# Fixing VectorE's order in the opening of an attention and GEGLU kernel, and storing its first values from SyncE

## The chip, the cores and the metric

The kernel runs on one core of a Trainium2 chip. A core has five engines that each work through their own list of instructions in order and meet at semaphores: TensorE (PE, matrix products), VectorE (DVE, elementwise work on whole tiles), ScalarE (ACT, activations and copies), GpSimd (POOL) and SyncE (SP, here only a queue that issues transfers). ACT and POOL issue transfers too, from the same list as their other work. The metric is device time in microseconds for one execution; the number of a version is the median of its runs.

## The reference

With S = 2048 tokens, D = 512 channels, F = 1792 hidden channels, 32 heads of 16 channels, all float32:

```python
q, k, v = split(x @ wqkv)                     # 32 heads of 16
idx = pos[:, None] - 2 * arange(8)[None, :]   # 8 keys, every second token back
attn = softmax(where(idx >= 0, einsum(q, k[idx]) / 4, -1e9))
a = einsum(attn, v[idx]) @ wo
b = (gelu(x @ w_gate) * (x @ w_up)) @ w_down
g = sigmoid((x * gate_w).sum(-1))
out = g * a + (1 - g) * b
```

A token attends only to tokens of its own parity (even or odd), so the two parities, 1024 tokens each, are independent of each other.

## The kernel before

**Stages.** The kernel does parity 0, then parity 1. Each parity has: the products for keys and queries, the products for values, 14 steps of the feed-forward part (`ffn`, f = 0 to 13), and the attention of four units of eight heads, which runs on VectorE in between (`scores`, `softmax`, `mix`), pulled in by credit as PE's work is written down.

**Seven products.** A product of x with a weight is cut into 2 x 2 blocks on both sides and done with seven block products instead of eight. The operands are blocks (`a11`, `a12`, `a22`, `b11`, `b12`, `b21`, `b22`) and sums of them: on the side of x, s1 = a21 + a22, s3 = a11 - a21, s2 = s1 - a11, s4 = a12 - s2 (`sum_x`, L237 to L242); on the side of the weight t3 = b22 - b12, t2 = b11 + t3 up to the signs in the code, t4 and t1 (`combine_b`, L230 to L233, for keys; `make_v`, L157 to L185, for values). For keys and queries the order of the products is in `KEYS` (L449): a11·b11, a12·b21, s2·t2, s3·t3, a22·t4, and later s1·t1 and s4·b22.

**Two halves of a number.** Every operand is split in a rounded `hi` (written by ACT, L86 or L126, or by a DVE cast) and a rest `lo` = value - hi (DVE, L87, in `split`). A block product is hi·hi + lo·hi + hi·lo over two channel chunks (kc = 0, 1): six matmuls for each of four token tiles (t = 0 to 3), 24 in all, 512 columns wide for keys (L458, `key_mm`), 258 for values (L345, in `values`). So before PE can do the third product, DVE must have done, for each kc, three sums of x, one split of s2, two sums of weights and one split of t2, and ACT the two `hi` between them.

**The opening.** L1053 to L1066 load and split the first blocks. Then stand, in the order of the code: the first two key products (L1078 to L1085); `take_first` (L317 to L326), which copies the finished tile out of PSUM, t = 0 and 2 by DVE, t = 1 and 3 by ACT, and stores it with two transfers from SP; two steps of `make_v` (the split of the value weights b11 and b21); the operands of s2·t2 (L1095 to L1101); the value products 0 and 1 (L1102); the splits of s3 and t3; `third(2)`, `third(3)`, `third(4)` (L1108 to L1139), which do the third to fifth key product; and `values(0, ..., range(2, 7))` (L1170), the other five value products.

**Stores of values.** In `values`, `store` (L354) sends a tile of 128 x 256 to DRAM: 16 transfers in each parity, four of them after value product 1, eight after product 5, four after product 6. For parity 0 they stand in ACT's list, for parity 1 in SP's.

**Zeros.** L1142 to L1144 write 16 small blocks of zeros to DRAM from POOL, after `third(4)`.

**What sets the order.** The code above is not the order in which an engine gets its instructions. The framework's scheduler puts each engine's instructions in an order of its own, by dependences, priorities and an estimate of durations. Two calls bind it: `keep_in_program_order(ins)` keeps marked instructions of an engine in the order of the code among themselves, and `paced` (L574) ties an instruction behind the last matmul written so far. Before the change only the first casts (L1051) are marked. Transfers of SP's and ACT's queues share eight semaphores in turn, and most of them wait in the program for the transfer eight places before them.

**Parity 1.** `keys` (L414) writes the key products of parity 1 and pulls their operands step by step out of `prepare`, which begins with `urgent` (L253 to L268): the same operands of s2·t2 as in the opening, then the splits of s3.

Of the kernel before, what the change touches and what calls it, by code (L numbers as in the profile page):

```python
# [13 lines left out]
OP = mybir.AluOpType  # L14
# [30 lines left out]
def tile_gated_mix(ctx: ExitStack, tc: tile.TileContext, xt, wqkv, wff, wo, out):  # L45
# [36 lines left out]
    def split(eng, hi, lo, raw, copy=None, pinned=False):  # L82
        if copy:
            copy(hi, raw)
        else:
            nc.scalar.activation(hi, raw, AF.Copy)  # L86
        ins = eng.tensor_tensor(lo, raw, hi.bitcast(F32), op=OP.subtract)  # L87
        if pinned:
            tc.keep_in_program_order(ins)


    KS, VS, QS, OS, WS, DS = {}, {}, {}, {}, {}, {}
# [64 lines left out]
    def make_v():  # L157

        def parts(n):
            split(nc.vector, *VO[n], VR[n])  # L160
            VS_W[n] = dram.tile([2, P, VW], F32, name=f"vw{n}")
            keep_v.append(n)

        def sub(o, x, a, b):
            nc.vector.tensor_tensor(VR[x], VR[a], VR[b], op=OP.subtract)
            VR[o] = VR[x]

        parts("b11")
        yield
        parts("b21")  # L170
        yield
        sub("t1", "b11", "b12", "b11")
        parts("t1")
        yield
        parts("b22")
        yield
        sub("t3", "b12", "b22", "b12")
        sub("t2", "b22", "b22", "t1")
        parts("t2")
        yield  # L180
        sub("t4", "b21", "b21", "t2")
        yield
        for n in "t3", "t4":
            parts(n)
            yield  # L185
# [67 lines left out]
    def urgent():  # L253

        room_b("t2")
        for kc in range(2):
            for n in "s1", "s3", "s2":
                sum_x(kc, n)
            split_s("s2", kc)
            yield  # L260
            combine_b("t3", "b12", "b22", "b12", kc)
            combine_b("t2", "b11", "t3", "b11", kc, OP.add)
            split_b("t2", kc)
            yield
        MADE.add("t2")
        for kc in range(2):
            split_s("s3", kc)
            yield  # L268
# [48 lines left out]
    def take_first(ps, jj, copy):  # L317

        if not KQ:
            KQ.append(pool.tile([P, 3 * NP - 1, UC], F32, name="kq"))  # L320
        st = tl(next(stages))[:, :CU].rearrange("p (a d) -> p a d", a=2)
        two = ps.rearrange("p (a c d) -> p c a d", a=2, c=2)
        copy(KQ[0][:, NP - 1 + jj::NP], two[:, 0])
        copy(st, two[:, 1])
        for a, t in enumerate((KS[0, 0][1, W:], QS[0, 0][1])):
            nc.sync.dma_start(t.rearrange("(p j) d -> j p d", j=NP)[jj], st[:, a])  # L326

# [5 lines left out]
    def values(par, bg, step, ks=range(7)):  # L333

        C, Z_, PS, US, ST = {}, {}, {}, {}, {}

        def mm(ps, t, a, b, start):
            ts = slice(t * P, (t + 1) * P)
            for kc in range(2):
                ah, al = XOP[a, kc]  # L340
                for i, (x, w) in enumerate(((ah, 0), (al, 0), (ah, 1))):
                    first = start and kc == i == 0

                    n = 512 if first and a == "s1" else WQ
                    LAST[:] = [nc.tensor.matmul(ps[:, :n], x[:, ts], VO[b][w][:, kc * WQ:kc * WQ + n], start=first,  # L345
                                                stop=(kc == 1 and i == 2), skip_group_check=True)]

        def stage():
            return tl(next(stages))[:, :512]

        def copy(o, i):
            nc.scalar.activation(o, i, AF.Copy)  # L352

        def store(st, jj, hh):  # L354
            queue = nc.sync if par else nc.scalar
            queue.dma_start(rows(VS[par, hh][:, W:], jj), st.rearrange("p (c d) -> p c d", c=2))

        for k, (a, b) in enumerate((("a11", "b11"), ("a12", "b21"), ("s1", "t1"), ("s4", "b22"), ("s2", "t2"),
                                    ("s3", "t3"), ("a22", "t4"))):
            if k not in ks:  # L360
                continue
            for t in range(BT):
                if k == 0:
                    C[t] = bank(f"acc{t}") if par else bank("p")
                elif k == 1 and not par:
                    Z_[t] = C[t]
                elif k == 2:
                    Z_[t] = bank("p")
                    if not par:
                        C[t] = bank(f"acc{t}")  # L370
                        copy(C[t][:, :WQ], VB.pop(t))
                ps = Z_[t] if 0 < k < 4 else C[t]
                mm(ps, t, a, b, k in (0, 2))
                if k == 0 and par:
                    Z_[t] = bank("p")
                    copy(Z_[t][:, :WQ], ps[:, :WQ])
                elif k == 0:
                    VB[t] = tl("s" if t else "r")[:, :WQ]
                    copy(VB[t], ps[:, :WQ])
                elif k == 2:  # L380
                    PS[t] = stage()
                    copy(PS[t][:, :CU], ps[:, :CU])
                elif k == 3:
                    copy(PS[t][:, CU:], ps[:, :CU])
                elif k == 4:
                    US[t] = stage()
                    copy(US[t][:, CU:], ps[:, :CU])
                elif k == 5:
                    copy(US[t][:, :CU], ps[:, :CU])
                    nc.vector.tensor_tensor(PS[t], PS[t], US[t], op=OP.add)  # L390
                    store(PS[t][:, CU:], t, 1)
                    store(PS[t][:, :CU], BT + t, 1)
                else:
                    if k == 1 or not par:
                        ST[t] = stage()
                    jj, st = (t, ST[t][:, :CU]) if k == 1 else (BT + t, ST[t][:, CU:])
                    copy(st, ps[:, :CU])
                    copy(z[:, par, jj:jj + 1], ps[:, CU:WQ - 1])
                    store(st, jj, 0)
                next(bg, None)  # L400
                pull((0.77, 0.75)[par])
            step(k)
        for _ in bg:
            pass
        if 6 not in ks:
            return
        done.add((par, 1))
        en = pool.tile([P, 64], F32, name="en")[:, :NP]
        nc.scalar.activation(en, z[:, par], AF.Exp, scale=-1.0)
        nc.vector.tensor_scalar_add(en, en, 1.0)  # L410
        nc.vector.reciprocal(g[:, par], en)
        nc.vector.tensor_scalar(gc[:, par], g[:, par], -1.0, 1.0, op0=OP.mult, op1=OP.add)
# [160 lines left out]

    def paced(ins):  # L574

        if not PACING[0]:
            return ins
        tc.add_manual_dep(ins.ins, LAST[-1].ins.name, mybir.DependencyInfo(mybir.DependencyClass.Sync,
                          mybir.DependencyReason.SCHED_ONLY), reason="pace")
        return ins  # L580
# [472 lines left out]
    for kc in range(KC):  # L1053
        name, i = ("b11", "b21")[kc // 2], kc % 2
        if not i:
            room_b(name)
        first = ((0, P), (P, 512 - P)) if not kc else ((0, 512),)
        raw = QR[name, i] = spare[i] if kc > 1 else tl("rt")
        (nc.sync if kc else nc.scalar).dma_start(raw, wqkv[0, kc // 2, :, i * 512:i * 512 + 512])
        for a, n in first:  # L1060
            o = kc // 2 * 512 + a
            nc.sync.dma_start(XR[i][:, o:o + n], xt[0, :, kc, a:a + n])
        for c in first:
            split_x(0, 0, kc, (c,), None if kc else in_order)
            if not c[0]:
                split(nc.vector, *QO[name, i], raw)  # L1066
    set_x(0)
    for kc in range(2):
# [14 lines left out]
    for kc in range(2):  # L1083
        for t in range(BT):
            key_mm(Z_[t], t, *KEYS[1], (kc,), False)  # L1085
    for t in range(BT):
        take_first(Z_[t], t, first_copy[t % 2])
    room_v(*SMALL)
    made = make_v()
    for _ in range(2):  # L1090
        next(made)
    room_b("t2")
    S1.update((kc, pool.tile([P, UH, NP, W], F32, name="lg", bufs=2).rearrange("p h j w -> p (h j w)"))
              for kc in range(2))
    for kc in range(2):  # L1095
        for n in "s1", "s3", "s2":
            sum_x(kc, n)
        split_s("s2", kc)
        combine_b("t3", "b12", "b22", "b12", kc)
        combine_b("t2", "b11", "t3", "b11", kc, OP.add)  # L1100
        split_b("t2", kc)  # L1101
    values(0, iter(()), lambda k: None, range(2))  # L1102
    room_b("t3")
    for kc in range(2):
        split_s("s3", kc)
# [30 lines left out]
    next(made)  # L1136
    for f in range(2):
        fetch(f)
    third(4)  # L1139
    done.add((0, 0))  # L1140
    PACING[0] = True
    for t in (*KS.values(), *VS.values()):  # L1142
        for c in range(2):
            paced(nc.gpsimd.dma_start(t[c, :W], zero))  # L1144

    def first():
        for _ in range(2):
# [87 lines left out]
```

## Time and profile before

| | us |
|---|---|
| median of 3 runs | 623.32 (622.73 to 623.71) |
| the profiled execution | 622.21 |
| its span, first to last instruction | 620.4 |

| engine | busy us | share of the span |
|---|---|---|
| PE | 597.5 | 96% |
| DVE | 540.7 | 87% |
| ACT | 432.5 | 70% |
| POOL | 110.5 | 18% |

The mean granted clock of PE over the span is 0.983 of full speed. A row of the timeline gives the start and duration of an instruction (or of several equal ones, with their count), the engine, the line of the code, the operation, the tile written and the tiles read, and in brackets how long the engine sat idle before it and what ended that. A "q" behind an engine's name is that engine's list issuing a transfer. Line numbers are those of the kernel before. A row of the windows gives, for a stretch of time, each engine's busy time with its number of instructions, the granted clock of PE, and the load of the transfer engines.

### The profile page before, as it was taken

The numbers are of one execution on the slowest core, as the hardware profiler recorded it, in microseconds if no ns is written. First come the engines' busy times: TensorE is split into PE (matmuls) and PEld (weight loads), VectorE is DVE, ScalarE is ACT, GpSimd is POOL, SyncE is SP. The second block draws the span as 40 slices with busy tenths as digits, with TensorE's granted clock in tenths as the row PEclk, the third lists the DMA queues.
The fourth block names the chain that finished last, engine by engine and source line by source line (L and its number), as shares of the span: only waits on it lengthen the run. The fifth ranks groups of instructions, "written<-read, shape, count | busy, mean of one in ns | idle before, by whom it ended". The sixth has DMA issues, their size and how long they took to land.

```text
span 620.4 us, 8250 instructions
## 1 busy us (share of the span) xinstructions
PE 597.5 (96%) x2743; PEld 494.7 (80%) x2743; DVE 540.7 (87%) x637; ACT 432.5 (70%) x755; POOL 110.5 (18%) x129
## 2 busy tenths in 40 slices
PE   8798987999999999999889999999999999999997
PEld 7686876888878888887669988888888888888886
DVE  6937965999969998899978999899989998999892
ACT  6756489667797777886857666676687668686732
POOL 0006066111111111111200176011111111121300
PEclk9989988999999999999979999999999999999999
DMA  8677799988776967799849999968867896888824
GB/s 306 221 216 191 221 243 294 214 218 245 218 192 165 293 200 225 194 276 314 257 138 277 330 262 248 313 172 233 234 169 185 229 257 165 208 216 213 113 49 169
DMA packets 94697, 137.78 MB, mean 222 GB/s; under 512 B 8640, under 2 KB 58944, under 8 KB 94655
## 3 DMA queue, kind: packets, MB, share of 16 engines
q1 hardware_dynamic: 70510, 102.98, 50.6%
q0 software_dynamic: 19504, 31.79, 29.5%
q10 hardware_dynamic: 4640, 2.49, 1.4%
q8 instruction: 21, 0.34, 0.2%
q14 instruction: 22, 0.17, 0.1%
HBM read 69.83 MB, written 44.66 MB: 185 GB/s over the span
## 4 chain that ended last, share of the span: by engine, by line
PE 65%; DVE 13%; issue 8%; ACT 6%; DMA 6%; SPq 1%; ACTq 0%; POOL 0%; DVEq 0%; POOLq 0%
PE p L725 31%; PE acc L767 9%; PE p L767 8%; PE acc L458 7%; PE p L992 5%; PE p L345 2%; PE acc L992 2%; DVE prod L551 1%; PE acc L345 1%; DVE raw L242 1%; DMA raw<-xt 1%; DVE prod L511 1%; DMA vs<-hl 1%; DVE lg L514 1%; DMA r<-wff 1%
## 5 line engine op out<-in xcount | busy, mean ns | idle before, releaser
L725 PE MATMUL p<-S,g 128*128 128x512 f32 x672 | 170.6, 391 | 0.5 <-ACT s L730 0.5
L725 PEld LDWEIGHTS p<-S,g 128*128 128x128 f32 x672 | 126.7, 189 | 27.2 <-ACT s L730 0.9
L725 PE MATMUL p<-A,g 128*128 128x512 f32 x504 | 127.2, 391 | 4.6 <-ACT c L736 4.6
L725 PEld LDWEIGHTS p<-A,g 128*128 128x128 f32 x504 | 94.2, 188 | 25.5 <-ACT c L736 5.9
L511 DVE TENSOR_TENSOR prod<-kq 128x2048 f32<-128x2048 f32 x32 | 72.9, 2279 | 2.7 <-DMA kq<-kq 2.6
L551 DVE TENSOR_TENSOR prod<-v,lg 128x2048 f32<-128x2048 f32 x32 | 72.9, 2279 | 0.6
L514 DVE TENSOR_REDUCE lg<-prod 128x128 f32<-128x2048 f32 x32 | 73.0, 2282 | 0.1
L767 PE MATMUL p<-d,hh 128*128 128x512 f32 x224 | 69.2, 390 | 0.0
L683 POOL DMA_DIRECT2D g<-raw x28 | 24.6, 879 | 224.0 <-ACT g L680 134.9
L767 PE MATMUL acc<-d,hh 128*128 128x512 f32 x224 | 59.0, 389 | 0.0
L736 ACT ACTIVATE c<-p 128x512 f32<-128x512 f32 x56 | 33.4, 596 | 35.8 <-PE p L725 35.7
L767 PEld LDWEIGHTS acc<-d,hh 128*128 128x128 f32 x224 | 42.2, 188 | 8.9
L767 PEld LDWEIGHTS p<-d,hh 128*128 128x128 f32 x224 | 41.9, 188 | 9.2 <-ACT p L761 0.6
L744 DVE TENSOR_TENSOR hl<-c,hh 128x512 fp32r<-128x512 f32 x56 | 38.4, 687 | 6.8 <-ACT hh L743 6.8
L767 PE MATMUL p<-d,hl 128*128 128x512 f32 x112 | 42.8, 389 | 0.0
L741 DVE TENSOR_TENSOR c<-c 128x512 f32<-128x512 f32 x56 | 38.3, 683 | 5.0 <-ACT c L833 5.0
L737 DVE TENSOR_TENSOR c<-c,s 128x512 f32<-128x512 f32 x56 | 38.1, 685 | 4.7 <-ACT c L736 4.0
L716 POOL DMA_DIRECT2D d<-r x23 | 19.7, 858 | 123.4 <-ACT d L715 102.8
L458 PE MATMUL acc<-d,S 128*128 128x512 f32 x144 | 37.6, 410 | 2.4 <-ACT z L352 2.4
L743 ACT ACTIVATE hh<-c 128x512 fp32r<-128x512 f32 x56 | 35.0, 627 | 6.1 <-DVE c L741 5.9
L730 ACT ACTIVATE s<-p 128x512 f32<-128x512 f32 x56 | 33.0, 592 | 8.9 <-PE p L725 8.5
L555 DVE TENSOR_TENSOR prod<-prod 128x1024 f32<-128x1024 f32 x32 | 39.0, 1220 | 0.2
(207 smaller groups left out, 1047.0 us busy)
## 6 DMA issues: line engine op xcount, KB each, us to landing
g<-raw POOLq DMA_DIRECT2D x28, 512.0 KB, 6.1
raw<-wff SPq DMA_DIRECT2D x42, 256.0 KB, 4.2
ws<-g SPq DMA_DIRECT2D x14, 768.0 KB, 5.6
g<-ws SPq DMA_DIRECT2D x14, 768.0 KB, 6.8
r<-wff SPq DMA_DIRECT2D x28, 256.0 KB, 4.0
d<-r POOLq DMA_DIRECT2D x23, 256.0 KB, 6.7
v<-vs SPq DMA_DIRECT2D x8, 512.0 KB, 8.6
os<-tb SPq DMA_DIRECT2D x64, 64.0 KB, 4.5
```

The lines of the kernel that those rows point to most:

```text
L458: LAST[:] = [nc.tensor.matmul(ps, x[:, ts], w, start=(start and kc == i == 0), stop=(kc == 1 and i == 2), skip_group_check=True)]
L511: paced(nc.vector.tensor_tensor(prod, spans(k, jj), q[:, jj:jj + 2, None, :].to_broadcast([P, 2, W, UC]), op=OP.mult))
L514: nc.vector.tensor_reduce(two_of(lg, jj), prod.rearrange("p j w (h d) -> p (j w) h d", d=DH), axis=AX.X, op=OP.add)
L551: paced(nc.vector.tensor_tensor(prod.rearrange("p j w (h d) -> p (j w) h d", d=DH), spans(v, jj).rearrange("p j w (h d) -> p j w h d", d=D ...
L555: nc.vector.tensor_tensor(prod[:, :, :4], prod[:, :, :4], prod[:, :, 4:], op=OP.add)
L725: LAST[:] = [nc.tensor.matmul(ps, w_, a_, start=(start and kc == 0 and n == 0), stop=(kc == 1 and n == 2), skip_group_check=True)]
L737: nc.vector.tensor_tensor(c, c, s, op=OP.add)
L741: nc.vector.tensor_tensor(ge, ge, up, op=OP.mult)
L743: nc.scalar.activation(hh_, ge, AF.Copy)
L744: nc.vector.tensor_tensor(hl_, ge, hh_.bitcast(F32), op=OP.subtract)
L767: LAST[:] = [nc.tensor.matmul(pp, a[:, ts], w, start=(i == 0 and n == 0 and gr == 0), stop=(i == 1 and n == 2), skip_group_check=True)]
L992: LAST[:] = [nc.tensor.matmul(pa, a, b, start=(first and n == 0), stop=(last and n == 2), skip_group_check=True)]
```

## The change

Four things. VectorE's splits, sums and `take_first` copies of the opening, from the first loads to the end of `third(4)`, are marked to stay in the order of the code (`PIN[0]`), and the code is put in another order: the third product's operands for kc = 0 come first, then two of the `take_first` copies and the two splits of value weights, and so on; two more steps of `make_v` stand ahead of `third(4)`. In `urgent` (parity 1) the sums and splits of each kc are marked in the same way. The 16 blocks of zeros are written after value products 0 and 1 instead of after `third(4)`. The stores of values of parity 0 stand in SP's list instead of ACT's.

```diff
         ins = eng.tensor_tensor(lo, raw, hi.bitcast(F32), op=OP.subtract)
-        if pinned:
+        if pinned or PIN[0]:
             tc.keep_in_program_order(ins)
+
+    PIN = [False]
...
         def sub(o, x, a, b):
-            nc.vector.tensor_tensor(VR[x], VR[a], VR[b], op=OP.subtract)
+            paced(nc.vector.tensor_tensor(VR[x], VR[a], VR[b], op=OP.subtract))
             VR[o] = VR[x]
...
         room_b("t2")
         for kc in range(2):
+            PIN[0] = True
             for n in "s1", "s3", "s2":
                 sum_x(kc, n)
             split_s("s2", kc)
-            yield
+            PIN[0] = False
+            yield
+            PIN[0] = True
             combine_b("t3", "b12", "b22", "b12", kc)
             combine_b("t2", "b11", "t3", "b11", kc, OP.add)
             split_b("t2", kc)
+            PIN[0] = False
             yield
...
-        copy(KQ[0][:, NP - 1 + jj::NP], two[:, 0])
-        copy(st, two[:, 1])
+        paced(copy(KQ[0][:, NP - 1 + jj::NP], two[:, 0]))
+        paced(copy(st, two[:, 1]))
...
         def store(st, jj, hh):
-            queue = nc.sync if par else nc.scalar
-            queue.dma_start(rows(VS[par, hh][:, W:], jj), st.rearrange("p (c d) -> p c d", c=2))
+            nc.sync.dma_start(rows(VS[par, hh][:, W:], jj), st.rearrange("p (c d) -> p c d", c=2))
...
     def paced(ins):
 
+        if PIN[0] and ins.ins.engine == mybir.EngineType.DVE:
+            tc.keep_in_program_order(ins)
         if not PACING[0]:
             return ins
...
+        PIN[0] = True
+        if kc:
+            split(nc.vector, *QO[name, i], raw)
         for c in first:
             split_x(0, 0, kc, (c,), None if kc else in_order)
-            if not c[0]:
+            if not kc and not c[0]:
                 split(nc.vector, *QO[name, i], raw)
...
-    for t in range(BT):
-        take_first(Z_[t], t, first_copy[t % 2])
     room_v(*SMALL)
     made = make_v()
-    for _ in range(2):
-        next(made)
     room_b("t2")
...
     for kc in range(2):
         for n in "s1", "s3", "s2":
             sum_x(kc, n)
+        if not kc:
+            for t in range(2):
+                take_first(Z_[t], t, first_copy[t % 2])
+            for _ in range(2):
+                next(made)
         split_s("s2", kc)
         combine_b("t3", "b12", "b22", "b12", kc)
         combine_b("t2", "b11", "t3", "b11", kc, OP.add)
         split_b("t2", kc)
+        if not kc:
+            for t in range(2, BT):
+                take_first(Z_[t], t, first_copy[t % 2])
     values(0, iter(()), lambda k: None, range(2))
+    PACING[0] = True
+    for t in (*KS.values(), *VS.values()):
+        for c in range(2):
+            paced(nc.gpsimd.dma_start(t[c, :W], zero))
+    PACING[0] = False
...
     for f in range(2):
         fetch(f)
+    next(made)
+    next(made)
     third(4)
+    PIN[0] = False
     done.add((0, 0))
     PACING[0] = True
-    for t in (*KS.values(), *VS.values()):
-        for c in range(2):
-            paced(nc.gpsimd.dma_start(t[c, :W], zero))
```

## The prediction

> **What bounds the kernel now.** I read the busy times of the page first, then the windows, cut where PE changes its pace.
>
> ```profile
> PE 597.5 (96%) x2743; PEld 494.7 (80%) x2743; DVE 540.7 (87%) x637; ACT 432.5 (70%) x755; POOL 110.5 (18%) x129
> ```
> ```profile
> core 0: us, PE busy (x) PEld busy (x) DVE busy (x) ACT busy (x) POOL busy (x), PEclk, DMA share, GB/s
> ...
> 25.50:34.10 8.60, 5.08 (x14) 3.48 (x14) 8.60 (x16) 7.29 (x13) 0.00 (x0) 0.70 0.33 113
> ...
> 70.60:79.50 8.90, 6.52 (x28) 4.78 (x26) 8.87 (x8) 0.17 (x1) 0.00 (x0) 1.00 1.02 325
> 79.50:87.00 7.50, 7.46 (x26) 5.98 (x27) 4.18 (x4) 7.09 (x12) 4.91 (x4) 0.77 0.89 188
> 87.00:99.60 12.60, 12.58 (x56) 10.09 (x54) 7.46 (x16) 12.50 (x20) 10.37 (x9) 1.00 1.13 309
> 99.60:107.70 8.10, 4.63 (x13) 3.68 (x14) 5.36 (x10) 6.78 (x10) 4.29 (x5) 0.79 1.19 261
> ...
> 120.00:290.00 170.00, 168.86 (x744) 139.03 (x743) 159.24 (x191) 130.96 (x213) 19.72 (x23) 1.00 0.80 227
> ...
> 308.10:313.80 5.70, 1.47 (x5) 0.68 (x5) 5.70 (x11) 4.01 (x8) 0.00 (x0) 0.86 1.05 299
> 313.80:321.00 7.20, 7.20 (x21) 5.73 (x22) 3.02 (x6) 1.71 (x4) 0.00 (x0) 0.64 0.05 15
> ```
>
> From 120 to 290 PE is busy 168.86 of 170 us at full clock: there PE is the bound, and a microsecond saved earlier moves everything up. The loss sits in three places: an opening starved by DVE (25.5 to 41), a stretch starved by ACT (70 to 108), and the third key product of parity 1 (308 to 321). PE's timeline gives their size.
>
> ```profile
> 16.85 3.74 PE L345 MATMUL p<-c,A 128*128 128x258 f32 x30
> ...
> 28.16 1.49 PE L458 MATMUL acc<-g,S 128*128 128x512 f32 x4 [2.65 <-ACT S L126]
> 30.52 3.78 PE L458 MATMUL acc<-g,S 128*128 128x512 f32 x8 [0.87 <-DVE S L87]
> 34.10 6.39 PE L458 MATMUL acc<-d,S 128*128 128x512 f32 x24
> ...
> 69.75 0.76 PE L345 MATMUL acc<-c,A 128*128 128x258 f32 x5
> ...
> 79.54 7.35 PE L458 MATMUL acc<-d,S 128*128 128x512 f32 x24 [2.42 <-ACT z L352]
> 86.73 1.52 PE L725 MATMUL p<-S,g 128*128 128x512 f32 x6
> ...
> 103.07 2.17 PE L725 MATMUL p<-A,g 128*128 128x512 f32 x6 [3.49 <-ACT c L736]
> 107.51 0.85 PE L767 MATMUL acc<-d,hh 128*128 128x512 f32 x3
> ...
> 311.45 1.47 PE L458 MATMUL acc<-g,S 128*128 128x512 f32 x4 [3.37 <-ACT S L126]
> 313.80 7.26 PE L458 MATMUL acc<-g,S 128*128 128x512 f32 x20 [0.88 <-DVE S L87]
> 320.89 5.60 PE L458 MATMUL acc<-d,S 128*128 128x512 f32 x24
> 326.33 5.60 PE L458 MATMUL acc<-g,A 128*128 128x512 f32 x24
> ```
>
> At full clock 24 matmuls of 512 columns take 326.33 - 320.89 = 5.44 us (0.227 each); those of 258 columns take 3.74/30, about 0.12. Each wait is paid twice, since the clock falls behind it: the 24 from 79.54 took 7.19 us (1.75 too many), the 12 from 103.07 took 4.44 instead of 2.72 (1.72), the 20 from 313.80 took 7.09 instead of 4.53 (2.56). The opening's 36 from 25.5 to 40.49 took 15 us instead of 8.2, of which 3.5 is idle and 3.3 clock.
>
> **The opening.** DVE's and ACT's rows give the prices.
>
> ```profile
> 12.04 0.69 DVE L242 TENSOR_TENSOR lg<-raw 128x512 f32<-128x512 f32 x1 [0.57 <-DMA raw<-xt]
> ...
> 13.37 0.69 DVE L87 TENSOR_TENSOR A<-raw,A 128x512 fp32r<-128x512 f32 x1
> ...
> 18.26 0.42 DVE L323 COPY kq<-p 128x256 f32<-128x256 f32 x1
> 18.59 0.41 DVE L324 COPY hh<-p 128x256 f32<-128x256 f32 x1
> ...
> 23.14 0.69 DVE L87 TENSOR_TENSOR g<-rt,g 128x512 fp32r<-128x512 f32 x1
> 23.74 0.69 DVE L242 TENSOR_TENSOR raw<-raw 128x512 f32<-128x512 f32 x1
> ...
> 42.73 0.42 DVE L323 COPY kq<-acc 128x256 f32<-128x256 f32 x1 [6.55 <-PE acc L458]
> ```
> ```profile
> 14.01 0.64 ACT L86 ACTIVATE c<-v 128x516 fp32r<-128x516 f32 x1 [0.78 <-DMA v<-wqkv]
> ```
>
> A 512-column DVE instruction takes 0.60 us from start to start in a stream (23.14 to 23.74), a copy 0.33, a `hi` on ACT 0.64. The old order mixes in work that nobody needs yet (the a22 split at 13.37, sums for t3, t4 and the values), and then DVE stands idle 6.55 us at 42.7. The changed order, from the built program, moves that work behind. Walking it from 12.04:
>
> - kc = 0: three sums to 13.9, the copies of tile 0 to 14.6, the value splits at 14.7 and 16.3 (the second waits for its `hi`, fifth in ACT's list from 14.01), the s2 split, two sums to 18.8, then 1 us of waiting for ACT: t2's `lo` at 19.75.
> - kc = 1: copies, three sums to 22.9; s2's `hi` stands behind ACT's copies of value tiles that PE finishes at 23.0, so its `lo` comes at 24.2; two sums to 26.1, `hi` to 27.05, `lo` right behind.
> - PE: 30 value matmuls from 16.85, 8 of the key product, 18 values, 4 keys, done at 25.3; it waits 1.75 us for the `hi` of 27.05 and does the last 12 by 29.8, against 34.1. The s3·t3 operands are ready at 30.1, so this product ends near 35.3, against 40.5; a22·t4 near 40.75.
> - The marked order puts the value sums behind all key operands, and ACT's `hi` of the value operand t1 stands behind its copy of the last a22·t4 tile: ready at 41.75, a new wait of 1.0 us. Then 120 value matmuls (eight first ones 512 wide, 0.1 more each) and the 12 of the feed-forward that stand between them: 14.4 + 0.8 + 2.7 = 17.9, to 59.7.
>
> The old kernel finished the values at 70.5 with 27 feed-forward matmuls between them, 15 more, 3.4 us; like for like 67.1. **Gain 7.4 us.** The zeros leave POOL before its first transfer for f = 0; that transfer is covered by value products, so I give them nothing (at most the 0.5 us by which it may be late).
>
> **The stores.**
>
> ```profile
> 71.67 6.64 DMA vs<-hl
> ```
> ```profile
> 79.32 0.17 ACT L352 ACTIVATE z<-acc 128x1 f32<-128x1 f32 x1 [8.90 <-DMA vs<-hh]
> ...
> 81.30 1.28 ACT L817 ACT_TABLE_LOAD   x1
> ...
> 106.65 1.28 ACT L833 ACT_TABLE_LOAD   x1
> ```
> ```profile
> 75.20 0.39 SPq L641 DMA_DIRECT2D raw<-wff  x1
> ```
> ```profile
> DMA to landing us min/median/max: 1.8/4.7/11.5
> ```
>
> The first line is the chain of waits. A store that waits for an earlier transfer to land holds ACT's whole list: 8.90 us in which ACT makes no copy. Then ACT, 99% busy from 87 to 99.6, works off its arrears, with seven table loads from 81.30 to 106.65. PE pays 2.42 + 1.75 + 3.49 + 1.72 = 9.4 us. In the changed program ACT issues none of these stores and has three loads in the same steps (17 in the whole program instead of 23): 8.9 + 4 x 1.28 = 14 us less for ACT here, more than the arrears. The wait itself moves to SP. Behind the last store there stands the fetch of f = 2's weights (issued at 75.20 before). On the same walk the twelve stores are ready from 58.9 to 62.5 and stand with three others, 15 transfers at some 0.5 us, to 66.5; PE needs f = 2 only 108 matmuls (24.5 us) after 59.7, at 84. A landing of 4.7, even 11.5, plus about 8 for combining and splitting leaves it in time. I take 1.5 us as left over: **gain 7.9 us**; bounds 0 (SP late by the whole arrears) and 9.4.
>
> **The third key product of parity 1.**
>
> ```profile
> 282.94 0.60 ACT L736 ACTIVATE c<-p 128x512 f32<-128x512 f32 x1 [2.62 <-PE p L725]
> ```
> ```profile
> 285.75 0.68 DVE L737 TENSOR_TENSOR c<-c,s 128x512 f32<-128x512 f32 x1
> ...
> 304.63 0.68 DVE L232 TENSOR_TENSOR hh<-hh 128x512 f32<-128x512 f32 x1
> ```
>
> From the addition at 285.75 to the first operand sum DVE had 18.9 us of work. The new order has 3.2 us more attention there, but puts the addition ahead of a long attention product, at 283.55: first sum at 305.65. Three sums, `hi`, `lo`, two sums, a t3 split, `hi`: PE can start kc = 0 at 310.75 and ends its 12 at 313.5. For kc = 1 two s3 splits, not marked, have slipped between the sums, and t2's `hi` comes at 317.7: 4.2 us idle, then 12 matmuls, 320.4 against 320.9. So a gain of 0.5 at full clock, and with the clock down (12 x 0.227 more) a loss of 2.2. The nearest row is this product's own, where a wait of 3.37 cost 2.56 of clock: I take the **loss of 2.2**.
>
> The Trainium skill, "TensorE: Matmul & The Clock Gate", Part 1, says that PE falls to half rate after an idle window of about 3.4 us that runs freely. By it the 4.2 us wait that the change makes halves the rate, as I took it, and the 1.75 and 1.0 us waits of the opening do not; in the rows above a wait of 2.42 was enough. By the rule the allowance for the opening in the next line would fall away and the time be 611.0.
>
> **The sum.** For the clock behind the 1.75 us wait I take off 1.0 (bounds 0 and the 3.3 of the old opening), for SP's fuller list 0.8. 7.4 + 7.9 - 2.2 - 1.0 - 0.8 = 11.3. The span of 620.4 becomes 609.1; the profiled run adds 1.8 around it (622.21), 610.9; the median of the runs is 1.1 above that run: **612.0 us**.
>
> **The rivals.**
> - *SP takes ACT's place.* Its list stands still as ACT's did, f = 2 and f = 3 come late, and the stretch from 70 to 108 stays as it is: 612.0 + 7.9 - 0.8 = 619.1. For it: the transfer engines' share is 0.89 to 1.19 from 70 to 108. Against it: 17 us of lead.
> - *The clock falls in the opening too.* The new waits of 1.75 and 1.0 cost what the old ones did, 3.3 instead of 1.0: 614.3. For it: the old 0.88 us wait at 313.80 stood in a stretch at 0.64. Against it: both are shorter than every wait that began such a stretch.
> - *No change.* The lead is given back: DVE, 94% busy from 120 to 290, becomes the bound and the time stays within 1.2 us of 623.3. Against it: the order carries no more work into these steps, only the same, up to 4.4 us later.
> - *Slower.* The other order of all later steps of parity 0 puts a 2.2 us attention instruction ahead of an addition PE waits for. A step has 66 matmuls, 15 us, and DVE 159.24/170 of that, so 0.9 us of slack; if 12 steps lose 1.4 us beyond it, 16.8 us: 612.0 + 16.8 = 628.8. It decides from 0.95 us per step. Against it: the same rules of order lost 1.1 us there in all.
>
> **How the numbers follow.** Forecast 0.60, SP 0.15, clock 0.12, no change 0.04, slower 0.09. A measurement of this kernel tells about 0.2% (1.2 us) from no change. Faster is 0.60 + 0.15 + 0.12 = 0.87, same 0.04, slower 0.09. The forecast's own range is 606 (none of the two allowances, 1.8; a full clock in parity 1, 2.7; none of the 1.5 left over) to 616 (half of the stores' gain lost); taking in the clock and SP cases gives 605.5 to 619.5.
>
> **What would show it.** Right: s2·t2 done near 29.8, values near 60; ACT without a wait over 3 us from 55 to 90; PE idle under 3 us in all from 60 to 100; parity 1's third product with two waits, the second near 4 us. Wrong: SP's fetch of f = 2 landing after 78; a PE idle of 1 us or more per step from 100 to 270; the granted clock below 0.9 from 25 to 45.

## The result, and the profile after

The changed kernel takes 616.82 us (median of 4 runs, 614.32 to 617.15) beside 623.52 for the old one on the same chip: a ratio of 0.9885 (95% interval 0.9856 to 0.9913), 6.7 us faster. Measured a second time on another chip (below, with TensorE's order) it was 0.9902 (0.9867 to 0.9937). 612.0 was forecast, a gain of 11.3; the time lies above the forecast's own range of 606 to 616 and inside the wider one, which ends at 619.5. The profiled execution took 617.15 us, its span 615.4, 5.0 less than the old one's 620.4. Lines are now those of the changed kernel: L463 was L458 (key products), L351 was L345 (values), L732 was L725 and L774 was L767 (feed-forward part), L690 was L683 (the weights' accumulating transfer on GpSimd), L437 and L440 were L432 and L435 (copies of key tiles in `keys`), L782 was L775 (the scaled output of the feed-forward part), L128 was L126 (`held`), L358 was L352 (ScalarE's copies of value tiles), L477 was L472 (its copies of key and query tiles), L468 and L469 were L463 and L464 (GpSimd's stores of them), L234 and L244 were L232 and L242 (VectorE's sums).

The page's first part and the windows of the changed kernel, cut where PE changes its pace (columns as in the prediction's windows):

```profile
PE 594.9 (97%) x2743; PEld 494.5 (80%) x2743; DVE 542.8 (88%) x637; ACT 423.6 (69%) x749; POOL 110.4 (18%) x129
```
```profile
20.00:41.00 21.00, 19.68 (x94) 15.57 (x92) 15.88 (x26) 13.61 (x32) 8.37 (x16) 1.00 0.62 178
...
60.00:90.00 30.00, 29.80 (x131) 24.14 (x130) 29.01 (x34) 19.45 (x35) 19.43 (x17) 1.00 1.13 279
90.00:100.50 10.50, 5.96 (x28) 4.60 (x26) 8.96 (x13) 5.55 (x9) 2.06 (x2) 0.92 1.13 297
100.50:106.00 5.50, 5.50 (x14) 4.37 (x15) 2.09 (x2) 2.51 (x3) 0.86 (x1) 0.53 1.19 242
...
120.00:290.50 170.50, 170.50 (x753) 140.96 (x752) 162.03 (x191) 127.70 (x211) 20.68 (x26) 1.00 0.81 230
290.50:315.10 24.60, 16.58 (x52) 12.04 (x50) 17.89 (x24) 12.82 (x24) 2.17 (x4) 0.79 0.54 166
```

Two of the three old holes are smaller: the opening runs at full clock, and from 60 to 90 PE has 29.80 of 30 us. What is left are a hole at 90 to 106, close to the old one at 99.6 to 107.7 but with another cause, and a wider one at the start of parity 1 (290.5 to 315.1). PE's timeline of the changed kernel, first the opening:

```profile
25.78 0.98 PE L351 MATMUL p<-c,A 128*128 128x258 f32 x6 [1.26 <-ACT s L358]
26.82 3.02 PE L463 MATMUL acc<-g,S 128*128 128x512 f32 x12
29.84 5.73 PE L463 MATMUL acc<-d,S 128*128 128x512 f32 x24
35.42 5.60 PE L463 MATMUL acc<-g,A 128*128 128x512 f32 x24
42.01 2.17 PE L351 MATMUL p<-g,S 128*128 128x512 f32 x12 [0.99 <-ACT g L86]
...
59.66 1.53 PE L732 MATMUL p<-S,g 128*128 128x512 f32 x6
```

s2·t2 is done at 29.84, s3·t3 at 35.42, the wait for the value operand t1 is 0.99 us, and the values end at 59.66. The wait of 1.26 us is not the one that was forecast: it stands before six value matmuls and ends with a copy of a value tile on ScalarE, while the `hi` forecast for 27.05 is done at 26.76, before PE gets to it. Then the hole at 90 to 106, on PE and in the chain of waits:

```profile
100.48 1.22 PE L732 MATMUL p<-A,g 128*128 128x512 f32 x2 [4.54 <-DMA g<-raw]
...
103.21 2.69 PE L732 MATMUL p<-S,g 128*128 128x512 f32 x6
```
```profile
70.52 5.63 DMA raw<-wff
...
85.33 15.11 DMA g<-raw
```

PE waits 4.54 us for a transfer of GpSimd's that was issued at 85.33 and took 15.11 us, and behind it six matmuls take 2.69 us (1.53 for the six at 59.66). The weights themselves are in time (fetched at 70.52, landed at 76.15). Its neighbours in GpSimd's queue, from the list of transfers between 60 and 110 us (count, size, median us from issue to landing), and below them transfers of its own kind between 110 and 260:

```profile
ks<-rt POOLq DMA_DIRECT2D x8, 128.0 KB, 12.4
...
g<-raw POOLq DMA_DIRECT2D x10, 512.0 KB, 6.2
```

GpSimd's timeline has the first of these stores of key and query tiles; the last is issued at 89.88:

```profile
67.56 1.22 POOL L468 DMA_DIRECT2D ks<-rt  x1 [8.86 <-ACT rt L477]
```

The transfer stands in one queue with the sixteen accumulating stores of key and query tiles, twelve of them issued before it; away from them such a transfer takes 6.2 us at the median. But the old kernel had the same transfer in much the same crowd. These are its rows there, from GpSimd's timeline, from the list of transfers issued between 94 and 95 us, and from PE's timeline:

```profile
94.51 1.21 POOL L683 DMA_DIRECT2D g<-raw  x1
```
```profile
g<-raw POOLq DMA_DIRECT2D x1, 512.0 KB, 14.4
```
```profile
111.16 0.84 PE L725 MATMUL p<-A,g 128*128 128x512 f32 x3
```

It was issued at 94.51, behind ten of the sixteen stores, and landed 14.4 us later, at 108.9. The first matmul that needs it is the 105th of the feed-forward part's first products (L725, now L732) in both kernels. The old kernel reached it with the third matmul of the row at 111.16, at 111.6, with 2.7 us to spare. The changed kernel is ready for it at 100.48 - 4.54 = 95.94, 15.7 us earlier, while the transfer is issued only 9.2 us earlier and takes 0.7 us longer. So the transfer is late because PE's need moved further forward than the transfer did. ScalarE's longest wait from 55 to 90 is now this one:

```profile
66.67 1.09 ACT L477 ACTIVATE rt<-acc 128x512 f32<-128x512 f32 x2 [2.83 <-PE acc L463]
```

Last, the start of parity 1: PE, then ScalarE, then VectorE.

```profile
289.96 1.07 PE L774 MATMUL p<-d,hl 128*128 128x512 f32 x4
294.39 8.45 PE L463 MATMUL p<-d,A 128*128 128x512 f32 x24 [3.36 <-ACT p L437]
303.21 3.02 PE L463 MATMUL acc<-g,S 128*128 128x512 f32 x12 [0.37 <-ACT g L128]
310.53 4.57 PE L463 MATMUL acc<-g,S 128*128 128x512 f32 x12 [4.30 <-ACT g L128]
315.09 5.75 PE L463 MATMUL acc<-d,S 128*128 128x512 f32 x24
```
```profile
290.39 0.69 ACT L782 ACTIVATE s<-p,gc 128x512 f32<-128x512 f32 x1 [4.86 <-PE p L774]
...
293.73 2.07 ACT L437 ACTIVATE p<-acc 128x512 f32<-128x512 f32 x4
...
301.52 0.60 ACT L440 ACTIVATE rt<-p 128x512 f32<-128x512 f32 x1 [1.01 <-PE p L463]
302.02 0.62 ACT L128 ACTIVATE d<-hh 128x512 fp32r<-128x512 f32 x1
```
```profile
293.81 2.28 DVE L519 TENSOR_REDUCE lg<-prod 128x128 f32<-128x2048 f32 x1
296.01 2.13 DVE L244 TENSOR_TENSOR raw<-raw 128x512 f32<-128x512 f32 x3
...
302.67 0.69 DVE L87 TENSOR_TENSOR d<-hh,d 128x512 fp32r<-128x512 f32 x1 [1.82 <-ACT d L128]
```

The third product's two waits are there, the second 4.30 us. Unforecast is the 3.36 us wait before the second product: the last four matmuls of the feed-forward part (289.96) now stand last, with no key matmul behind them, and ScalarE needs from 290.39 to 293.73 to free their banks before it makes the copies that PE waits for. In the old kernel 18 key matmuls covered the same copies.

A ruler for all runs: the work of PE up to the second key product of parity 1 (L463, `p<-d,A`) is the same in every version, so the moment at which PE has done it (the product's start less its wait) shows the lead, and the time from there to s3·t3 (48 matmuls, 10.9 us at full clock) shows what the start of parity 1 costs. Old: 302.48 and 18.4. Changed: 294.39 - 3.36 = 291.03, a lead of 11.45, and 315.09 - 291.03 = 24.1. So 5.6 of the 11.45 us are given back there.

### The profile page after: what moved, and what is told of

It reads as the page before. It is cut to its first block, busy times and chain, and to the rows that moved or that the text cites. A ratio compares the mean times of both kernels' runs of the same rounds, so it can differ in the third digit from the quotient of the medians.

```text
span 615.4 us, 8243 instructions
## 1 busy us (share of the span) xinstructions
PE 594.9 (97%) x2743; PEld 494.5 (80%) x2743; DVE 542.8 (88%) x637; ACT 423.6 (69%) x749; POOL 110.4 (18%) x129
## 4 chain that ended last, share of the span: by engine, by line
PE 85%; DMA 5%; issue 4%; ACT 2%; DVE 1%; POOL 1%; SPq 0%; POOLq 0%; DVEq 0%; ACTq 0%
PE p L732 38%; PE p L774 12%; PE acc L774 11%; PE acc L463 9%; PE p L999 4%; PE acc L351 3%; PE p L351 3%; DMA g<-raw 2%; PE p L463 2%; PE acc L999 2%; DMA raw<-wff 1%; DMA S<-raw 1%; DMA raw<-os 1%; PE p L72 1%; ACT S L128 0%
## 5 line engine op out<-in xcount | busy, mean ns | idle before, releaser
L732 PE MATMUL p<-S,g 128*128 128x512 f32 x672 | 169.6, 391 | 0.0
L732 PEld LDWEIGHTS p<-S,g 128*128 128x128 f32 x672 | 126.7, 189 | 26.2
L732 PE MATMUL p<-A,g 128*128 128x512 f32 x504 | 126.7, 392 | 4.5 <-DMA g<-raw 4.5
L732 PEld LDWEIGHTS p<-A,g 128*128 128x128 f32 x504 | 94.7, 189 | 24.6 <-DMA g<-raw 5.0
L774 PE MATMUL p<-d,hh 128*128 128x512 f32 x224 | 68.4, 390 | 0.0
L690 POOL DMA_DIRECT2D g<-raw x28 | 24.2, 865 | 238.6 <-ACT g L687 106.5
L774 PE MATMUL acc<-d,hh 128*128 128x512 f32 x224 | 59.6, 389 | 0.2 <-ACT rt L477 0.2
L774 PEld LDWEIGHTS acc<-d,hh 128*128 128x128 f32 x224 | 42.1, 188 | 9.3 <-ACT rt L477 0.6
L774 PEld LDWEIGHTS p<-d,hh 128*128 128x128 f32 x224 | 42.1, 188 | 9.0 <-ACT p L768 0.3
L774 PE MATMUL p<-d,hl 128*128 128x512 f32 x112 | 42.8, 389 | 0.0
L787 ACT ACTIVATE rt<-p 128x512 f32<-128x512 f32 x48 | 28.4, 596 | 12.6 <-PE p L774 12.1
```

The lines of the kernel that those rows point to most:

```text
L732: LAST[:] = [nc.tensor.matmul(ps, w_, a_, start=(start and kc == 0 and n == 0), stop=(kc == 1 and n == 2), skip_group_check=True)]
L774: LAST[:] = [nc.tensor.matmul(pp, a[:, ts], w, start=(i == 0 and n == 0 and gr == 0), stop=(i == 1 and n == 2), skip_group_check=True)]
```

## The experiments

All edits are against the changed kernel unless said otherwise.

**Each half alone.** First the stores back on ScalarE, then, in the old kernel, only the stores moved.

```diff
         def store(st, jj, hh):
-            nc.sync.dma_start(rows(VS[par, hh][:, W:], jj), st.rearrange("p (c d) -> p c d", c=2))
+            queue = nc.sync if par else nc.scalar
+            queue.dma_start(rows(VS[par, hh][:, W:], jj), st.rearrange("p (c d) -> p c d", c=2))
```

> The changed kernel with parity 0's value stores back in ScalarE's list. Theory A (the two parts of the change are worth what their own stretches show): the opening keeps its 7.4 us, values end near 60 plus whatever PE does between them, ScalarE waits some 9 us for a transfer again and PE pays about 9 us between 65 and 108; at the start of parity 1 the last four matmuls of the feed-forward part again have 18 key matmuls behind them, so no wait before the second key product, and the third loses 2.2 to its pinned order: 623.5 - 7.4 + 2.2 = 618.3. Rival B (ScalarE's block ends when a transfer lands, whatever came before, so the opening's lead is swallowed there): 625.7.

Measured: 620.0 (10 runs), ratio 0.996 (0.9933 to 0.9987). Its profiled execution was the fastest of the ten, so I ran it once more:

> The first run's kernel again, since its profiled execution (616.67) was the fastest of its ten (median 620.0) and one profile cannot size the two parts. Theory A (the parts overlap: the order alone already takes most of what ScalarE's block costs): k = 1 of parity 1 starts again 7 to 9 us before the old kernel's, median 618 to 620. Rival B (that execution was a lucky one, ScalarE's block is usually paid in full): PE loses 8 us or more between 65 and 115 and the second key product starts only 4 to 6 us before the old kernel's.

Measured: 619.1, ratio 0.9953 (0.9927 to 0.998); this time the profiled execution, 622.20, was among the slowest. PE's timeline of the second execution, and ScalarE's longest wait for a store there:

```profile
27.13 4.61 PE L464 MATMUL acc<-g,S 128*128 128x512 f32 x12 [1.90 <-ACT g L128]
...
294.74 5.60 PE L464 MATMUL p<-d,A 128*128 128x512 f32 x24
...
318.77 5.74 PE L464 MATMUL acc<-d,S 128*128 128x512 f32 x24
```
```profile
72.31 0.17 ACT L358 ACTIVATE z<-acc 128x1 f32<-128x1 f32 x1 [4.54 <-DMA vs<-hh]
```

The time is nearer to A, in both. Three things follow. The store that holds ScalarE holds it 4.54 us (5.76 in the first execution) and not 8.90: an earlier opening alone already takes part of the block, and the lead at the second key product is 302.48 - 294.74 = 7.7 us, 9.5 in the other execution. The opening is 1.4 to 1.9 us worse than in the changed kernel, because PE's order leaves no value matmuls behind the wait, which is 1.90 us and followed by a slow clock (4.61 against 3.02 for the same twelve). And there is no wait at all before the second key product, yet from there to s3·t3 it takes 318.77 - 294.74 = 24.0 us (22.5 in the other), as much as in the changed kernel: the 3.36 us wait is not what costs.

> The old kernel with only parity 0's value stores moved to SyncE. Theory A: ScalarE has no wait over 3 us from 65 to 100, but GpSimd's list then carries the sixteen key and query stores right before the accumulation for the third feed-forward step, PE waits 4 to 5 us for that, and the net gain is 4.2 of the old 9.4: 623.5 - 4.2 = 619.3. Rival B (that wait needs the earlier opening too): gain 7.9 to 9.4, 614.1 to 615.6. Rival C (SyncE takes ScalarE's place): 623.5.

Measured: 620.98 (10 runs), ratio 0.9996 (0.9974 to 1.0019), no gain that stands clear of the noise; the lead at the second key product is 2.35 us (301.67 - 1.54 = 300.13). The chain of waits, PE and SyncE's list:

```profile
93.90 16.07 DMA g<-raw
```
```profile
110.01 2.07 PE L724 MATMUL p<-A,g 128*128 128x512 f32 x4 [4.10 <-DMA g<-raw]
```
```profile
79.93 1.05 SPq L641 DMA_DIRECT2D raw<-wff  x1
```

The same transfer of GpSimd's, 16.07 us long, costs 4.10 us without the new opening, and ScalarE has no wait over 2.4 us from 65 to 100: both are as A said. But C, which gives the time, is there too. With the stores in its list SyncE fetches the last piece of f = 2's weights at 79.93, where the old kernel did at 75.63. They land at 87.2 (80.4 in the old kernel), and GpSimd's transfer is issued at 93.90, only 0.6 us before the old kernel's. Without the new opening SyncE takes a good part of ScalarE's place.

**Without the wait for GpSimd.** VectorE forms the second rest of f = 2.

```diff
-        if not i:
-            KEEP[f] = w[:, :2 * n]
+        if not i or (not par and f == 2):
+            if not i:
+                KEEP[f] = w[:, :2 * n]
```

> The changed kernel, but the rest of the third feed-forward step's second weight group (f = 2) is formed by VectorE instead of by a negated copy on ScalarE and an accumulating transfer on GpSimd's queue. Theory A (the 4.54 us wait at 96 to 100 is that transfer, stuck behind the key and query stores in GpSimd's queue, and the 0.53 clock behind it is its second payment of 2.1): wait gone, 616.8 - 6.6 = 610.2, less at most 1 for the work VectorE gets. Rival B (the weights themselves or their combination are late): the wait moves to VectorE, 614.5 to 617.

Measured: 612.36 (611.97 to 613.09), ratio 0.985 (0.9824 to 0.9876), 2 to 3 us under the changed kernel by the ratios (of its two measurements) and 4.5 by the medians. The time alone does not choose between A and B; the windows of this run do:

```profile
90.00:100.00 10.00, 10.00 (x45) 8.26 (x44) 8.91 (x16) 6.83 (x11) 3.14 (x3) 1.00 1.17 311
100.00:106.00 6.00, 6.00 (x28) 4.83 (x27) 5.90 (x7) 5.38 (x9) 1.08 (x2) 1.00 1.07 243
```

The hole is closed, at full clock, and the lead at the second key product rises from 11.45 to 17.4 us (288.43 - 3.35 = 285.08). So A holds in its place: the transfer is the cause of this hole. At the start of parity 1 0.7 us of the added lead goes again (309.83 - 285.08 = 24.75 to s3·t3).

> The fourth run's kernel (VectorE forms the rest of f = 2's second group) with parity 0's value stores in ScalarE's list: what the stores' move is worth once the wait for GpSimd's transfer is out of the way. The fourth run took 0.985 of the old kernel. Theory A (the move is worth its 7.9 us and the GpSimd wait ate most of it): 0.985 + 7.9/623 = 0.9975 or 621. Rival B (the order alone has taken most of it already): 2 to 4 us slower than the fourth run, 614.5 to 616.5.

Measured: 616.39 (615.65 to 617.07), ratio 0.99 (0.9867 to 0.9932), 3 to 4 us slower than the fourth run: B. With GpSimd's transfer out of the way moving the stores is worth about half of the forecast, and ScalarE's block in this run is 6.62 us. The lead at the second key product is 12.3 us, against 17.4 with the stores moved. Of the 5.1 us between them 1.7 are the opening's (the values end at 61.99 against 60.26) and 3.4 come behind it, where 7.1 were forecast.

**Parity 1 without the marks.** The two `PIN[0] = True` and `PIN[0] = False` pairs in `urgent` are taken out.

> The changed kernel without the marks on VectorE's sums and splits in urgent (parity 1). Theory A: PE's order there is as in the changed kernel, so the 3.4 us wait before the second key product stays; the third product loses its 4.3 us wait for the second chunk and gets a shorter one before the first; the marks cost 2.2, so 616.8 - 2.2 = 614.6. Rival B (the marks cause the whole loss of 5.8 at the start of parity 1, the wait before the second product too): 611.0. Rival C (the marks cost nothing): 616.8.

Measured: 613.72 (609.37 to 616.77), ratio 0.9866 (0.9804 to 0.9927). The time is too scattered to choose; PE's timeline isn't:

```profile
294.87 8.61 PE L459 MATMUL p<-d,A 128*128 128x512 f32 x24 [3.36 <-ACT p L433]
...
311.16 5.60 PE L459 MATMUL acc<-d,S 128*128 128x512 f32 x24
```

The wait before the second product stays, as A said, and from its earliest start to s3·t3 it takes 311.16 - 291.51 = 19.65 us. In the changed kernel this was 24.1, and 23.4 in its second execution below: between these executions the marks cost 3.7 to 4.4 us, where A said 2.2.

**The changed kernel again, and TensorE's order.** The second edit puts the last four matmuls of `keys`' first product behind the last four of the feed-forward part.

```diff
                 key_mm(ps, t, a, b, (1,) if k == 0 else (0, 1), False)
                 if k == 0:
+                    tc.add_manual_dep(LAST[0].ins, DOWN[-1].ins.name, mybir.DependencyInfo(
+                        mybir.DependencyClass.NoSync, mybir.DependencyReason.DATA), reason="down first")
...
+        if gr == NG - 1 and b and not par:
+            DOWN.append(LAST[0])
```

> The changed kernel once more, on the same chip as the next three, as the number to set them against: 0.9885 of the old kernel.

> The changed kernel with one order on TensorE: at the start of parity 1 the last four matmuls of the first key product stand behind the last four of the feed-forward part (in the changed kernel none do, in the old one eighteen did). Theory A (the wait before the second key product is ScalarE's chain of ten copies behind those last matmuls, but the third product's operands on VectorE set the end): that wait falls from 3.4 to about 2.4 us, the wait before the third product grows by as much, time within 1 us of the changed kernel. Rival B (that wait and the clock behind it are themselves paid): 2 to 4 us faster.

Measured: 616.45 (0.9902, 0.9867 to 0.9937) and 615.06 (0.9892, 0.9849 to 0.9936). PE's timeline of the changed kernel's second execution, then of the other order, whose profiled execution (618.28) was the slowest of its four:

```profile
294.09 7.06 PE L463 MATMUL p<-d,A 128*128 128x512 f32 x24 [3.36 <-ACT p L437]
...
308.83 5.41 PE L463 MATMUL acc<-g,S 128*128 128x512 f32 x12 [4.30 <-ACT g L128]
314.08 5.60 PE L463 MATMUL acc<-d,S 128*128 128x512 f32 x24
```
```profile
296.53 5.74 PE L466 MATMUL p<-d,A 128*128 128x512 f32 x24 [2.45 <-ACT p L440]
304.82 4.61 PE L466 MATMUL acc<-g,S 128*128 128x512 f32 x12 [2.56 <-ACT g L129]
312.06 4.60 PE L466 MATMUL acc<-g,S 128*128 128x512 f32 x12 [2.62 <-ACT g L129]
316.65 5.74 PE L466 MATMUL acc<-d,S 128*128 128x512 f32 x24
```

A: the wait before the second product falls to 2.45 us and the clock stays full, and the third product's waits grow by nearly as much (0.37 + 4.30 = 4.67 to 2.56 + 2.62 = 5.18). From the second product's earliest start to s3·t3 it is 22.6 us, beside 23.4 and 24.1 in the two executions of the changed kernel.

These two executions also show how much the stretch from 70 to 106 varies. GpSimd's transfer took 12.8 us in both, and PE waited 2.69 us for it in the changed kernel's second execution and 2.50 with the other order, instead of 4.54. With the other order, whose edit touches nothing ahead of parity 1, SyncE's fetch of f = 2's weights was late as well (the chain of waits, then PE):

```profile
74.38 8.10 DMA raw<-wff
```
```profile
87.45 1.22 PE L735 MATMUL p<-A,g 128*128 128x512 f32 x2 [2.52 <-ACT g L682]
```

They landed at 82.48, and PE waited 2.52 us for the operand made of them.

**Together.**

> The third and the fourth run's edits together (no marks in urgent; VectorE forms the rest of f = 2's second group). Their stretches lie 180 us apart with PE the bound between them, so theory A: they add, 4.1 us (third product of parity 1) and 4.8 us (96 to 106), some 9 us under the changed kernel. Rival B (the lead won at 100 is given back at the start of parity 1, whose wait is for VectorE): 4 to 5 us under it.

Measured: 609.80 (608.69 to 613.24), ratio 0.981 (0.9766 to 0.9853): 5.7 us under the changed kernel by the ratios and 6.65 by the medians, nearer to B. Here the start of parity 1 takes 308.48 - 285.80 = 22.7 us, 2.05 less than with the marks (24.75 in the run without the wait for GpSimd): PE has more lead and waits longer for VectorE. The last run goes at that:

```diff
         room_b("t2")
         for kc in range(2):
-            PIN[0] = True
+            PACING[0] = False
             for n in "s1", "s3", "s2":
                 sum_x(kc, n)
-            split_s("s2", kc)
-            PIN[0] = False
-            yield
-            PIN[0] = True
+                PIN[0] = True
             combine_b("t3", "b12", "b22", "b12", kc)
             combine_b("t2", "b11", "t3", "b11", kc, OP.add)
+            PIN[0] = False
+            PACING[0] = True
+            yield
+        for kc in range(2):
+            split_s("s2", kc)
+            PIN[0] = True
             split_b("t2", kc)
             PIN[0] = False
...
+        split_x(1, 1, 2, copy=held)
         yield
         again(0, 3)
+        split_x(1, 1, 3, copy=held)
         yield
...
-        for kc in (2, 3):
-            split_x(1, 1, kc, copy=held)
-            yield
```

The two splits of a22 stand earlier in `tail`; the sums and combinations of both chunks come before either split; a chunk's first sum carries no mark. The run also has the edits of the run without the wait for GpSimd and of TensorE's other order. The first sum is left free on the idea that a mark also ties it behind the attention instruction written just before it (the reduction at 293.81 above); no run tests that by itself.

> As the last, and at the start of parity 1: the splits of a22 earlier in the code, the sums of both chunks written one behind the other and bound only among themselves (not behind the attention written before them) and not paced, and the order on TensorE of the second run. Theory A (the 13 us that PE loses there are VectorE's and ScalarE's order): the third product's operands are ready about 5 us earlier, 603 to 606. Rival B (attention work that was put behind comes to stand in the way of the next products): as the last run.

Measured: 606.21 (604.66 to 611.15), ratio 0.9756 (0.9704 to 0.9808): faster than both kernels and nearer to A, though its interval still meets the last run's. PE's timeline, in the fastest of its four executions:

```profile
285.42 1.24 PE L781 MATMUL p<-d,hl 128*128 128x512 f32 x4 [2.06 <-DVE hl L758]
...
288.92 7.79 PE L469 MATMUL p<-d,A 128*128 128x512 f32 x24 [0.56 <-ACT p L443]
...
303.48 5.73 PE L469 MATMUL acc<-d,S 128*128 128x512 f32 x24
```

From 288.36 to s3·t3 it takes 15.1 us, 7.6 less than in the last run. But 2.6 of these only moved ahead of the ruler's point (288.36 beside 285.80): there PE has a new wait of 2.06 us for the last product of the feed-forward part, and a slower clock behind it. s3·t3 starts 5.0 us earlier than in the last run. Which of the edits at the start of parity 1 brings how much was not tried one by one.

## Why the prediction was right, and where its sizes were off

**The opening: right.** s2·t2 29.8 (29.84), s3·t3 35.3 (35.42), the wait of 1.0 (0.99), values 59.7 (59.66): 7.4 us like for like. (The old rows have 26 feed-forward matmuls before the values' end and not 27, which moves this by 0.1.) The wait taken as 1.75 did not come as such: PE's order put six value matmuls before the last twelve, and the 1.26 us were theirs. The clock stayed at 1.00, so the allowance of 1.0 was not needed. In part that was luck: the twin with the stores back on ScalarE has VectorE's same order, but none of these matmuls behind the wait, and it shows 1.90 us and a slow clock. The Trainium skill, "TensorE: Matmul & The Clock Gate", Part 1, which let that allowance fall away, agrees with the changed kernel (1.26 us, full clock) and not with the twin, whose 1.90 us is shorter than the page's window of 3.4 us.

**The stores: right in what they do, wrong in size.** ScalarE lost its waits, and in the profiled execution SyncE did not take its place (the weights of f = 2 landed at 76.15, before the 78 named as the limit, though their fetch went out at 70.5 and not at 66.5). But the term of 7.9 less 0.8, 7.1 net, measured 11.45 - 7.4 = 4.05 between the values' end and the second key product. The step that failed is "plus about 8 for combining and splitting". It fits the first group of f = 2's weights, which PE takes up at 84.15 without a wait. The second group goes through GpSimd's transfer, for which the sum has no term, although it took 14.4 us in the old profile: from landing to the last operand it was 100.44 - 76.15 = 24.3 us, 15.1 of them the transfer. "PE idle under 3 us in all from 60 to 100" fails by this one wait. Without it the stretch gains 10.6 us (17.4 less the 6.8 at a values' end of 60.26), more than the 9.4 counted in the old profile. How long the transfer takes is not explained: with ten to twelve stores before it it took between 10.2 and 16.07 us in eight executions, the transfer engines' share was 1.13 to 1.19 from 90 to 106 and 0.81 from 120 on, and neither moving the stores nor easing that load was tried.

A second error does not lower the sum but says whose gain it is. The term was taken from the old profile as if the earlier opening left ScalarE's block as it was. Without the move the stretch still gains 2.2 to 3.5 us (leads of 7.7 and 9.5, less 5.5 and 6.0 at the values' end, which comes at 61.56 and 61.09 there).

**The third key product of parity 1: right in sign, more than twice the size.** The wait forecast as 4.2 was 4.30, and the clock fell behind it. The loss was 5.6 us at the start of parity 1 (4.9 in the second execution), with 2.2 forecast. The step that failed is the walk along VectorE up to the first half of the product, in two places. The walk has the first sum at 305.65 before any lead; it came at 296.01, 9.6 us earlier, while PE's lead was 11.45, so VectorE was 1.8 us short. And from there to PE's start the walk has 5.1 us, but it took 303.21 - 296.01 = 7.2: VectorE waited 1.82 us for a `hi` (302.67), which stood in ScalarE's list behind the copy of a tile of the second key product (301.52), which waited for PE. A late or slow second product thus delays the operands of the third. That the executions of the changed kernel show the same 0.37 and 4.30 behind a second product of 8.45 and of 7.06 us fits this.

**The rivals.** The slower one and no change fell: from 120 to 290.5 PE is busy 170.50 of 170.50 us. The clock in the opening did not fall. SP taking ACT's place fell in the profiled execution, but not for good: with TensorE's other order the same list brought the weights at 82.48 and PE waited 2.52 us, and with the stores moved alone they came at 87.2. The stretch that this rival named, 70 to 108, stayed partly open in the changed kernel too, from 90 on, through GpSimd's queue.

**The balance.** 7.4 + 4.05 - 5.6 = 5.85, of which the span shows 620.4 - 615.4 = 5.0 (the rest is lost behind s3·t3 of parity 1); the forecast had 6.4 + 7.1 - 2.2 = 11.3. The wider range holds 616.82 only by the room left for a fallen clock and a late SP; what used it up was GpSimd's transfer and the start of parity 1. That the time fell inside is luck in this respect; the two gains and the one loss were foreseen where they came.

## What to carry to other kernels

When a stretch is pulled forward, list every operand that it needs with the time at which it lands, those made by other queues too: what had 2.7 us to spare is late as soon as the need moves further than the transfer. A loss read from an old profile is not a gain to be added if another part of the same change moves its start. Read the built order of every engine at a seam, TensorE's too: a chain of operands that is pinned on one engine still waits in the lists of the others.

## What was not expected of the hardware

One and the same wait is followed by different clocks. Behind 3.36 us of idle time the 24 matmuls took 8.45 us in one execution of the changed kernel and 7.06 in another (a row of 24 at full clock reads 5.60); behind 2.45 us in another version they took 5.74; behind 1.90 us twelve matmuls took 4.61 instead of 3.02. So "each wait is paid twice" is too much: these four waits are 11.1 us together, and the clock behind them cost 6.0. The Trainium skill, same page and part, says that the window runs freely and that the number of slow matmuls at a kernel's start varies between its runs. The two executions vary in the same way behind one and the same wait.

An accumulating transfer of 512 KB in GpSimd's queue took 6.2 us at the median where the queue was free of the stores, and 10.2 to 16.07 behind them (14.4 in the old kernel, 15.11 and 12.8 in the changed one), which themselves took 12.4 at the median for 128 KB each. The Trainium skill, "DMA: Bandwidth & Descriptors", Anatomy of one DMA — SWDGE (gpsimd) path, gives a fit of 2.0 us plus the bytes at 436 GB/s, 3.2 us for this size (an estimate worked out from that page); all of these are longer.
